# A recurrent attention and a gated feed-forward: inputs loaded by unit, smaller blocks at both ends, two fused operations

## The chip, the cores and the metric

The kernel runs on one core of one Trainium2 chip. The time is device time in microseconds (us) from launch to end. Before the change it is 272.43 us, the median of three runs (272.05 to 272.52). The core's engines each run their own stream of instructions in a fixed order: TensorE (PE; its weight loads are PEld), VectorE (DVE), ScalarE (ACT), GpSimd (POOL) and SyncE (SP), which issues transfers here; GpSimd issues the weight loads. An instruction waits at the head of its stream until the semaphores that it needs are set, and all that stands behind it in that stream waits too.

## The reference

```
# r, k, v, w: 4 x 8 heads x 768 steps x 48, float32; u: 8 x 48
for t in range(768):                       # for every batch and head
    cur   = outer(u * k[t], v[t])
    y[t]  = r[t] @ (state + cur)
    state = w[t][:, None] * state + outer(k[t], v[t])
x   = y as 3072 tokens x 384               # tokens of a batch in order, heads side by side
out = ((x @ w1) * (x @ w2)) @ w3 @ w_out   # 384 -> 1024 -> 1024 -> 384
```

## The kernel before, in words

Time is cut into chunks of 128 steps. A *unit* n is one chunk of one batch with all eight heads: there are 24 units, 6 for each of the 4 batches, and the state is handed from one unit of a batch to the next.

`prep` takes the logarithm of w (`lw`, on ScalarE) and a bf16 copy of v (`v_bf`, on GpSimd). `att_a` sums the logarithms along time with two triangular matrices on TensorE (`cs`, lines 137 to 139), takes the exponential of both sums (`e_sb`, line 140), multiplies k by the one and r by the other (`krt`, line 143, VectorE), transposes the eight pieces (`tr`, line 147) and copies them out of PSUM (`trs`, line 150). On GpSimd k, u and r are multiplied (`uk`, lines 153 and 154); VectorE sums over the head (`dsum`), and GpSimd multiplies that by v (`yd`): the part of a step with itself. `att_b` forms the 128 x 128 products of every head (`m`, line 174), masks them (`mbf`, line 177), forms the next state (`kv`, lines 183 and 186: two products a pair of heads, and behind each pair a one-column sum of the logarithms; then `pc`, `ts_`, `s_bd`, `s_f`), adds state and chunk parts into `y`, and transposes the result into `xT` (`yt`, lines 226 and 230).

The feed-forward works on blocks of four units (512 tokens). `ffn_ab` makes one group of 128 hidden columns: three matmuls into `a_ps`, three into `b_ps`, a copy of a on ScalarE and a product on VectorE into `abT` (line 250). `ffn_out` makes 128 tokens of the output with eight matmuls (`o_ps`) against `w34`, a copy and a store. `w34` is w3 @ w_out, made once in the kernel by `w34_transpose` (transposes of w3, lines 264 and 265) and `w34_mul` (line 270).

Loads: batch 0 comes chunk by chunk (24 loads of 192 KB on SP), batches 1 to 3 whole, four loads of 1.125 MB each, asked for at the first unit of the batch before, with two buffers for each input. GpSimd issues the weight loads, which turn float32 into bf16 on the way: w1 and w2 behind `att_a` of unit 0, w3 and w_out behind that of unit 1. `keep_in_program_order` pins each behind the GpSimd instruction written before it.

Order: the program writes units 0 to 3, then for each block j its feed-forward parts in four lots, with a unit of the next block ahead of each lot; for block 0 the making of w34 stands between a/b and out. The framework's scheduler then orders each engine's stream: of what its own model of the times takes to be ready it picks what was written first. So an instruction of a later unit can stand in a stream ahead of one of an earlier unit. Buffers bound how far ahead it gets: three for `lw`, `krt` and `v_bf`, two for most others.

PSUM has eight banks: three for the feed-forward (`ps_ffn`), two that `cs` (twice), `tr`, `kv` and `yt` share in turn (`ps_att`, tag att), two for the two halves of `m` (`ps_m`), one for `y`.

Of the kernel before, what the change touches and what calls it, by code (L numbers as in the profile page):

```python
# [14 lines left out]
def kernel(  # L15
# [48 lines left out]
    LT_incl = consts.tile([C, C], BF)  # L64
    LT_strict = consts.tile([C, C], BF)
# [34 lines left out]

    def load_batch(b, c0=0, c1=NC):
        for name, ap in (("w", w), ("k", k), ("r", r), ("v", v)):
            if c0 == 0:
                t = inp.tile([C, H, NC, D], F32, tag=name, name=f"{name}b", bufs=2)
                for c in range(NC):
                    ins[name, b, c] = t[:, :, c, :]
                bt[name] = t
            t = bt[name]
            if c1 - c0 == NC:
                nc.sync.dma_start(t.rearrange("t h c d -> t (h c) d"),  # L110
                                  ap[b].rearrange("h (c t) d -> t (h c) d", t=C))
            else:
                nc.sync.dma_start(t[:, :, c0, :], ap[b, :, c0 * C:c1 * C, :].rearrange("h t d -> t h d"))  # L113

    bt = {}
# [12 lines left out]

    state = {}

    def att_a(n):

        b, c = divmod(n, NC)
        lw = lws[n]
        v_bf = vbs[n]
# [100 lines left out]
    def ffn_ab(j, fi):  # L236
        if fi == 0:
            abts[j] = big.tile([P, FI, TB], BF, tag="abT", name=f"abT{j}")
        x = xts[j]
# [12 lines left out]
    def ffn_out(j, t):
# [6 lines left out]
        nc.sync.dma_start(out3[j * UPB + t], o_sb)

# [29 lines left out]
    def att(n):  # L290
        b, c = divmod(n, NC)
        if c == 0 and b + 1 < B:
            load_batch(b + 1)
# [2 lines left out]
        if n == 0:
            load_w(w1_bf, moe_w1)
            load_w(w2_bf, moe_w2)
        if n == 1:
            load_w(w3_bf, moe_w3)  # L300
            load_w(wo_bf, moe_w_out)
# [2 lines left out]
    fill = [lambda gi=gi: w34_transpose(gi) for gi in range(FI)] + \
           [lambda fi=fi: w34_mul(fi) for fi in range(FI)]
    for n in range(UPB):
        att(n)
    for j in range(NB):
        parts = [lambda fi=fi: ffn_ab(j, fi) for fi in range(FI)]
        if j == 0:  # L310
            parts += fill
        parts += [lambda t=t: ffn_out(j, t) for t in range(UPB)]
        units = [n for n in range((j + 1) * UPB, (j + 2) * UPB) if n < NU]
        k_ = 0
        for q in range(UPB):
            if q < len(units):
                att(units[q])
            e = len(parts) * (q + 1) // UPB
            while k_ < e:
                parts[k_]()  # L320
                k_ += 1


# [28 lines left out]
```

## Time and profile before

| | |
|---|---|
| median of three runs | 272.43 us |
| the profiled execution: time, span | 271.93 us, 270.2 us |
| mean granted clock of TensorE | 0.942 |
| busy: TensorE, VectorE, GpSimd, ScalarE | 204.8, 140.1, 111.6, 110.8 us |
| moved by DMA | 28.51 MB, mean 106 GB/s |

The span goes from the first to the last instruction; the time has the launch and the end around it. Busy is the time in which an engine has an instruction under way; matmuls are pipelined, so a busy TensorE is not one at its peak. The granted clock is the share of full speed that TensorE was given, with two levels, 1.2 and 2.4 GHz. Bytes of the weight loads count as they are written, in bf16.

### The profile page before, as it was taken

Reading aid. Unit: us, or ns where it says so; the run is one execution under the profiler, and the core shown is the slowest. Engines: PE = TensorE matmul, PEld = TensorE weight load, DVE = VectorE, ACT = ScalarE, POOL = GpSimd, SP = SyncE. Lnnn points to the kernel's source line nnn. Section 1 sums busy time; section 2 is a strip of 40 time slices with the busy share of each in tenths; the row PEclk is TensorE's granted clock in tenths of the full one; section 3 lists DMA queues with packets and bytes.
Section 4 is the critical chain, followed back from the end, with each engine's and each line's share of the span. In section 5 each row is a group of like instructions: output and inputs, shape, how many; then the busy total and the mean of one; then the engine's idle time right before and its main releaser. Section 6 shows DMA issues by size and latency. Waiting matters only on the chain.

```text
span 270.2 us, 4248 instructions
## 1 busy us (share of the span) xinstructions
PE 204.8 (76%) x1624; PEld 110.1 (41%) x1624; DVE 140.1 (52%) x246; ACT 110.8 (41%) x221; POOL 111.6 (41%) x152
## 2 busy tenths in 40 slices
PE   2460450359998859988897998959997699994994
PEld 1240230134465535534453444525454345552452
DVE  5340530543689323267776677666764646742340
ACT  3240210225444323345645564534655336442342
POOL 4762530861503953455474536754471313100000
PEclk9999999999999986999999999968999659996899
DMA  6999999999999992146919910300003000020003
GB/s 145 184 180 196 184 202 189 184 187 189 189 173 188 186 187 36 58 92 139 174 65 184 205 23 0 121 0 2 0 0 119 0 0 2 1 90 29 0 1 116
DMA packets 50084, 28.51 MB, mean 106 GB/s; under 512 B 25616, under 2 KB 48272, under 8 KB 50064
## 3 DMA queue, kind: packets, MB, share of 16 engines
q1 hardware_dynamic: 47184, 23.79, 45.2%
q0 software_dynamic: 2880, 4.46, 9.3%
q8 instruction: 12, 0.20, 0.3%
q14 instruction: 8, 0.07, 0.1%
HBM read 27.98 MB, written 4.72 MB: 121 GB/s over the span
## 4 chain that ended last, share of the span: by engine, by line
PE 48%; DVE 13%; POOL 10%; SPq 10%; DMA 9%; issue 4%; ACT 3%; POOLq 0%; ACTq 0%; DVEq 0%
PE a_ps L242 11%; PE b_ps L246 11%; SPq L113 10%; PE o_ps L255 8%; DMA vb<-in_v_dram 7%; DVE krt L143 5%; PE tr L147 4%; PE kv L183 3%; POOL yd L158 3%; DVE mbf L177 3%; POOL uk L154 2%; POOL uk L153 2%; PE m L174 2%; PE kv L186 2%; PE y L218 2%
## 5 line engine op out<-in xcount | busy, mean ns | idle before, releaser
L250 DVE TENSOR_TENSOR abT<-a_sb,b_ps 128x512 bf16<-128x512 f32 x48 | 32.9, 686 | 29.9 <-PE b_ps L246 27.4
L242 PE MATMUL a_ps<-xT,w_bf 128*128 128x512 bf16 x144 | 45.3, 415 | 0.7 <-ACT xT L230 0.6
L246 PE MATMUL b_ps<-xT,w_bf 128*128 128x512 bf16 x144 | 45.1, 404 | 0.4 <-ACT a_sb L249 0.4
L249 ACT COPY a_sb<-a_ps 128x512 f32<-128x512 f32 x48 | 28.2, 586 | 31.4 <-PE a_ps L242 30.2
L177 DVE TENSOR_TENSOR mbf<-m,mask 128x512 bf16<-128x512 f32 x48 | 30.8, 684 | 12.4 <-PE m L174 12.4
L150 ACT COPY trs<-tr 128x1024 bf16<-128x1024 bf16 x24 | 24.3, 1011 | 30.3 <-PE tr L147 27.4
L255 PE MATMUL o_ps<-w,abT 128*128 128x384 bf16 x192 | 36.6, 326 | 0.0
L153 POOL TENSOR_TENSOR uk<-kb,u_bc 128x384 f32<-128x384 f32 x24 | 26.4, 1104 | 18.6 <-DVE dsum L156 16.9
L156 DVE TENSOR_REDUCE dsum<-uk 128x8 f32<-128x384 f32 x24 | 13.2, 551 | 38.5 <-POOL uk L154 30.4
L147 PE MATMUL tr<-I,krt 128*128 128x128 bf16 x192 | 22.1, 248 | 11.1 <-DVE krt L143 10.7
L124 POOL CAST v_bf<-vb 128x384 bf16<-128x384 f32 x24 | 12.0, 504 | 41.5 <-DMA vb<-in_v_dram 19.4
L147 PEld LDWEIGHTS <-krt 128*128 128x128 bf16 x192 | 13.5, 109 | 36.4 <-DVE krt L143 33.5
L154 POOL TENSOR_TENSOR uk<-uk,rb 128x384 f32<-128x384 f32 x24 | 26.0, 1086 | 3.7 <-DMA rb<-in_r_dram 2.6
L140 ACT ACTIVATE e_sb<-cs 128x384 f32<-128x384 f32 x48 | 23.3, 496 | 4.5 <-PE cs L139 4.3
L218 PE MATMUL y<-v_bf,mbf 128*128 128x48 bf16 x192 | 13.7, 193 | 15.0 <-DVE mbf L177 15.0
L121 ACT ACTIVATE lw<-wb 128x384 bf16<-128x384 f32 x24 | 12.6, 525 | 28.5 <-DMA wb<-in_w_dram 28.5
L230 ACT COPY xT<-yt 128x384 bf16<-128x384 bf16 x24 | 11.5, 478 | 29.8 <-PE yt L226 29.7
L143 DVE TENSOR_TENSOR krt<-kb,e_sb 128x384 bf16<-128x384 f32 x24 | 15.6, 649 | 13.5 <-ACT e_sb L140 13.5
L158 POOL TENSOR_TENSOR yd<-v_bf,dsum 128x384 bf16<-128x384 bf16 x24 | 20.3, 846 | 5.0 <-DVE y_bf L223 4.3
L255 PEld LDWEIGHTS <-abT 128*128 128x128 bf16 x192 | 17.4, 97 | 10.6 <-DVE abT L250 0.2
L242 PEld LDWEIGHTS <-w_bf 128*128 128x128 bf16 x144 | 14.3, 104 | 17.9 <-issue 7.9
L183 PE MATMUL kv<-v_bf,krt 128*64 128x48 bf16 x160 | 19.6, 224 | 0.9 <-POOL v_bf L124 0.9
(100 smaller groups left out, 254.6 us busy)
## 6 DMA issues: line engine op xcount, KB each, us to landing
out_dram<-o_sb SPq DMA_DIRECT2D x24, 192.0 KB, 1.9
w_bf<-in_moe_w_dram POOLq DMA_DIRECT2D x1, 2048.0 KB, 15.2
w_bf<-in_moe_w_dram POOLq DMA_DIRECT2D x2, 768.0 KB, 9.8
wb<-in_w_dram SPq DMA_DIRECT2D x6, 192.0 KB, 4.8
kb<-in_k_dram SPq DMA_DIRECT2D x6, 192.0 KB, 7.6
rb<-in_r_dram SPq DMA_DIRECT2D x6, 192.0 KB, 6.4
vb<-in_v_dram SPq DMA_DIRECT2D x6, 192.0 KB, 5.0
wo_bf<-in_moe_w_out_dram POOLq DMA_DIRECT2D x1, 768.0 KB, 19.7
```

What stands on the lines that cost most here:

```text
L143: nc.vector.tensor_mul(krt[:, j, :, 0:D], ins["kr"[j], b, c], e_sb[:, j])
L147: nc.tensor.transpose(tr[:, j, p, :], krt[:, j, 2 * p:2 * p + 2, :].rearrange("t h d -> t (h d)"), I128)
L153: nc.gpsimd.tensor_mul(uk, ins["k", b, c], u_bc)
L154: nc.gpsimd.tensor_mul(uk, uk, ins["r", b, c])
L158: nc.gpsimd.tensor_mul(yd, v_bf, dsum[:, :, None].to_broadcast([C, H, D]))
L177: nc.vector.tensor_mul(mbf[:, q], mps[q], mask)
L183: nc.tensor.matmul(kv[q * DP:(q + 1) * DP, p, 0:D], lhsT=krt[:, 0, 2 * p + q, :], rhs=v_bf[:, 2 * p + q, :], start=True, stop=True)
L242: nc.tensor.matmul(a_ps, lhsT=w1_bf[:, di, fi * P:(fi + 1) * P], rhs=x[:, di, :], start=(di == 0), stop=(di == DI - 1))
L246: nc.tensor.matmul(b_ps, lhsT=w2_bf[:, di, fi * P:(fi + 1) * P], rhs=x[:, di, :], start=(di == 0), stop=(di == DI - 1))
L249: nc.scalar.copy(a_sb, a_ps)
L250: nc.vector.tensor_mul(abts[j][:, fi, :], a_sb, b_ps)
L255: nc.tensor.matmul(o_ps, lhsT=abts[j][:, fi, t * P:(t + 1) * P], rhs=w34[:, fi, :], start=(fi == 0), stop=(fi == FI - 1))
```

## The change

Inputs are loaded by unit: `load(n)` issues w, k, r and v of one unit into three tiles (k and r side by side in one), with eight buffers each. Units 0 to 7 are asked for at the start, unit n + 8 behind `att(n)`. w1 and w2 are issued behind unit 1's second `uk` product, w3 and w_out behind unit 3's, both under `high_priority`.

Blocks are lists of units: two of two units, four of four, two of two; the feed-forward of a block of two works on 256 columns. `big`, which holds `xT` and `abT`, gets three buffers.

The feed-forward parts form one list with an estimated cost each: a/b of blocks 0 and 1, w34, the outs of blocks 0 and 1, then a/b and out of each further block. Ahead of a part, units are written as long as their number is below 3 + (cost written so far)/4.1.

Both sums `cs` go into one tile of two banks (with -1 in the one triangle in place of the scale), one exponential and one product serve both. That tile and the `m` tile, now also of two banks, share one slot (`ps_m`, one buffer). `ps_att` keeps `tr`, `kv` and `yt`. The four one-column sums of `kv` stand behind its eight products.

```diff
-    NB = NTOK // TB
+    NIN = 8
+    BLOCKS = [(0, 2), (2, 4)] + [(n, n + 4) for n in range(4, NU - 4, 4)] + [(NU - 4, NU - 2), (NU - 2, NU)]
...
-    big = ctx.enter_context(tc.tile_pool(name="big", bufs=2))
+    big = ctx.enter_context(tc.tile_pool(name="big", bufs=3))
...
-    ps_m = ctx.enter_context(tc.tile_pool(name="ps_m", bufs=2, space=bass.MemoryType.PSUM))
+    ps_m = ctx.enter_context(tc.tile_pool(name="ps_m", bufs=1, space=bass.MemoryType.PSUM))
...
+    def load(n):
+        b, c = divmod(n, NC)
+
+        def src(ap):
+            return ap[b, :, c * C:(c + 1) * C, :].rearrange("h t d -> t h d")
+
+        w_in = inp.tile([C, H, D], F32, tag="w_in", name="w_in")
+        kr_in = inp.tile([C, 2, H, D], F32, tag="kr_in", name="kr_in")
+        v_in = inp.tile([C, H, D], F32, tag="v_in", name="v_in")
+        nc.sync.dma_start(w_in, src(w))
+        nc.sync.dma_start(kr_in[:, 0], src(k))
+        nc.sync.dma_start(kr_in[:, 1], src(r))
+        nc.sync.dma_start(v_in, src(v))
+        ins[n] = (w_in, kr_in, v_in)
...
+    def load_w(dst, ap):
+        with tc.high_priority():
+            d = nc.gpsimd.dma_start(dst, ap.rearrange("(i p) f -> p i f", p=P))
+        tc.keep_in_program_order(d)
...
-        for j, (lt, sc) in enumerate(((LT_incl, -1.0), (LT_strict, 1.0))):
-            cs = ps_att.tile([C, H, D], F32, tag="att")
-            nc.tensor.matmul(cs, lhsT=lt, rhs=lw[:, :, 0:D], start=True, stop=True)
-            nc.scalar.activation(e_sb[:, j], cs, Act.Exp, scale=sc)
+        cs = ps_m.tile([C, 2, TB], F32, tag="m", name="cs")
+        for j, lt in enumerate((LTn_incl, LT_strict)):
+            nc.tensor.matmul(cs[:, j, 0:DM], lhsT=lt, rhs=lw[:, :, 0:D], start=True, stop=True)
+        nc.scalar.activation(e_sb.rearrange("t j h d -> t j (h d)"), cs[:, :, 0:DM], Act.Exp)
         krt = kr_st[n % NS]
-        for j in range(2):
-            nc.vector.tensor_mul(krt[:, j, :, 0:D], ins["kr"[j], b, c], e_sb[:, j])
+        nc.vector.tensor_mul(krt[:, :, :, 0:D], kr_in, e_sb)
...
+        if n == 1:
+            load_w(w1_bf, moe_w1)
+            load_w(w2_bf, moe_w2)
+        if n == 3:
+            load_w(w3_bf, moe_w3)
+            load_w(wo_bf, moe_w_out)
...
-        mps = [ps_m.tile([C, HP, C], F32, tag="m", name=f"m{q}") for q in range(2)]
+        mps = ps_m.tile([C, 2, HP, C], F32, tag="m", name="mps")
...
+            for p in range(HP):
                 nc.tensor.matmul(kv[:, p, D:D + 1],
...
+        T = (BLOCKS[j][1] - BLOCKS[j][0]) * C
...
-    load_batch(0, 0, 1)
+    load(0)
     nc.sync.dma_start(u_bc, u.partition_broadcast(C))
-    for c in range(1, NC):
-        load_batch(0, c, c + 1)
+    for n in range(1, NIN):
+        load(n)
...
         att_b(n)
+        if n + NIN < NU:
+            load(n + NIN)
...
+    parts = []
+
+    def add_ab(j):
+        for fi in range(FI):
+            parts.append((1.3 * (BLOCKS[j][1] - BLOCKS[j][0]) / UPB, lambda fi=fi: ffn_ab(j, fi)))
+
+    def add_out(j):
+        for t in range(BLOCKS[j][1] - BLOCKS[j][0]):
+            parts.append((1.3, lambda t=t: ffn_out(j, t)))
+
+    add_ab(0)
+    add_ab(1)
+    for gi in range(FI):
+        parts.append((0.45, lambda gi=gi: w34_transpose(gi)))
+    for fi in range(FI):
+        parts.append((1.3, lambda fi=fi: w34_mul(fi)))
+    add_out(0)
+    add_out(1)
+    for j in range(2, len(BLOCKS)):
+        add_ab(j)
+        add_out(j)
+
+    lead, every = 3, 4.1
+    nxt, done = 0, 0.0
+    for cost, part in parts:
+        while nxt < NU and nxt < lead + done / every:
+            att(nxt)
+            nxt += 1
+        part()
+        done += cost
```

## Rows read from the trace of the kernel before

**Rows 1.** The page: busy us by engine; the chain that ended last, by engine.

```profile
PE 204.8 (76%) x1624; PEld 110.1 (41%) x1624; DVE 140.1 (52%) x246; ACT 110.8 (41%) x221; POOL 111.6 (41%) x152
...
PE 48%; DVE 13%; POOL 10%; SPq 10%; DMA 9%; issue 4%; ACT 3%; POOLq 0%; ACTq 0%; DVEq 0%
```

**Rows 2.** Windows by stage: window, its us, busy us by engine, PEclk, DMA share, GB/s.

```profile
0.00:64.00 64.00, 25.53 (x198) 14.78 (x198) 23.50 (x46) 15.58 (x31) 31.05 (x48) 1.00 1.10 183
108.00:208.00 100.00, 88.96 (x751) 47.19 (x750) 64.81 (x109) 52.25 (x106) 52.09 (x64) 0.97 0.34 79
12.00:28.00 16.00, 5.55 (x45) 3.27 (x45) 4.91 (x10) 3.50 (x7) 8.90 (x12) 1.00 1.12 186
28.00:48.00 20.00, 7.06 (x57) 4.16 (x58) 5.24 (x10) 2.86 (x6) 5.69 (x9) 1.00 1.18 195
48.00:96.00 48.00, 39.28 (x324) 22.23 (x323) 28.11 (x48) 20.00 (x40) 25.52 (x33) 1.00 1.05 184
180.00:200.00 20.00, 19.71 (x151) 9.68 (x150) 14.39 (x24) 11.33 (x24) 11.18 (x13) 0.89 0.00 1
```

**Rows 3.** Timeline, POOL: start us, us, engine, line, operation.

```profile
27.39 0.94 POOL L276 DMA_DIRECT2D w_bf<-in_moe_w_dram  x1
```

**Rows 4.** DMA issues: queue, count, KB each, median us to landing.

```profile
w_bf<-in_moe_w_dram POOLq DMA_DIRECT2D x2, 768.0 KB, 9.8
wo_bf<-in_moe_w_out_dram POOLq DMA_DIRECT2D x1, 768.0 KB, 19.7
```

**Rows 5.** Timeline, 26 to 51 us: waits of three engines, in brackets.

```profile
48.49 0.50 POOL L124 CAST v_bf<-vb 128x384 bf16<-128x384 f32 x1 [9.46 <-DMA vb<-in_v_dram]
49.70 0.52 ACT L121 ACTIVATE lw<-wb 128x384 bf16<-128x384 f32 x1 [13.90 <-DMA wb<-in_w_dram]
49.98 0.55 DVE L156 TENSOR_REDUCE dsum<-uk 128x8 f32<-128x384 f32 x1 [11.02 <-POOL uk L154]
```

**Rows 6.** Timeline, ACT: the 5th, 9th and 24th xT copy.

```profile
70.63 0.48 ACT L230 COPY xT<-yt 128x384 bf16<-128x384 bf16 x1 [0.66 <-PE yt L226]
...
120.14 0.48 ACT L230 COPY xT<-yt 128x384 bf16<-128x384 bf16 x1 [1.64 <-PE yt L226]
...
248.14 0.48 ACT L230 COPY xT<-yt 128x384 bf16<-128x384 bf16 x1 [3.56 <-PE yt L226]
```

**Rows 7.** Timeline, 138 to 146 us: one unit's cs, mbf, yt, next cs.

```profile
138.16 0.33 PE L139 MATMUL cs<-lw,LT_incl 128*128 128x384 bf16 x1
...
143.08 1.29 DVE L177 TENSOR_TENSOR mbf<-m,mask 128x512 bf16<-128x512 f32 x2 [1.99 <-PE m L174]
...
145.43 0.34 PE L226 MATMUL yt<-I,y_bf 128*128 128x128 bf16 x3 [0.65 <-DVE y_bf L223]
...
145.61 0.33 PE L139 MATMUL cs<-lw,LT_incl 128*128 128x384 bf16 x1
```

**Rows 8.** Timeline, PE: the first a_ps, the last b_ps and o_ps.

```profile
60.58 1.49 PE L242 MATMUL a_ps<-xT,w_bf 128*128 128x512 bf16 x3
...
260.29 0.81 PE L246 MATMUL b_ps<-xT,w_bf 128*128 128x512 bf16 x3
260.94 5.36 PE L255 MATMUL o_ps<-w,abT 128*128 128x384 bf16 x32
```

**Rows 9.** Timeline, PE, 225 to 230 us: kv and m in a dense stretch.

```profile
226.06 0.21 PE L183 MATMUL kv<-v_bf,krt 128*64 128x48 bf16 x2
...
227.00 0.38 PE L242 MATMUL a_ps<-xT,w_bf 128*128 128x512 bf16 x1
...
228.97 0.40 PE L174 MATMUL m<-trs 48*128 48x128 bf16 x8
229.30 0.34 PE L213 MATMUL y<-sbd,trs 128*128 128x96 bf16 x4
```

**Rows 10.** The page's groups: line, engine, operation, shapes, count, busy us, mean ns.

```profile
L249 ACT COPY a_sb<-a_ps 128x512 f32<-128x512 f32 x48 | 28.2, 586 | 31.4 <-PE a_ps L242 30.2
...
L140 ACT ACTIVATE e_sb<-cs 128x384 f32<-128x384 f32 x48 | 23.3, 496 | 4.5 <-PE cs L139 4.3
```

More of the change, by code (lines that the diff above doesn't have):

```diff
@@ L55 @@
     stat = ctx.enter_context(tc.tile_pool(name="static", bufs=1))
-    inp = ctx.enter_context(tc.tile_pool(name="inp", bufs=3))
+    inp = ctx.enter_context(tc.tile_pool(name="inp", bufs=NIN))
     work = ctx.enter_context(tc.tile_pool(name="work", bufs=2))
-    big = ctx.enter_context(tc.tile_pool(name="big", bufs=2))
+    big = ctx.enter_context(tc.tile_pool(name="big", bufs=3))
     ps_ffn = ctx.enter_context(tc.tile_pool(name="ps_ffn", bufs=3, space=bass.MemoryType.PSUM))
     ps_att = ctx.enter_context(tc.tile_pool(name="ps_att", bufs=2, space=bass.MemoryType.PSUM))
-    ps_m = ctx.enter_context(tc.tile_pool(name="ps_m", bufs=2, space=bass.MemoryType.PSUM))
+    ps_m = ctx.enter_context(tc.tile_pool(name="ps_m", bufs=1, space=bass.MemoryType.PSUM))
     ps_y = ctx.enter_context(tc.tile_pool(name="ps_y", bufs=1, space=bass.MemoryType.PSUM))
-    LT_incl = consts.tile([C, C], BF)
+    LTn_incl = consts.tile([C, C], BF)
     LT_strict = consts.tile([C, C], BF)
@@ L72 @@
     nc.vector.memset(ones_c, 1.0)
-    nc.gpsimd.memset(LT_incl, 1.0)
-    nc.gpsimd.affine_select(LT_incl, LT_incl, compare_op=Alu.is_ge, fill=0.0,
+    nc.gpsimd.memset(LTn_incl, -1.0)
+    nc.gpsimd.affine_select(LTn_incl, LTn_incl, compare_op=Alu.is_ge, fill=0.0,
                             base=0, channel_multiplier=-1, pattern=[[1, C]])
@@ L99 @@
     ins = {}
[L101 to L115, printed above, removed]
+    def load(n):
[10 more added lines that the diff above has]
+        ins[n] = (w_in, kr_in, v_in)
     vbs = {}
     def prep(n):
-        b, c = divmod(n, NC)
         lw = lw_st[n % NS]
-        nc.scalar.activation(lw[:, :, 0:D], ins["w", b, c], Act.Ln)
+        nc.scalar.activation(lw[:, :, 0:D], ins[n][0], Act.Ln)
         lws[n] = lw
         v_bf = work.tile([C, H, D], BF, tag="v_bf", bufs=3)
-        nc.gpsimd.tensor_copy(v_bf, ins["v", b, c])
+        nc.gpsimd.tensor_copy(v_bf, ins[n][2])
         vbs[n] = v_bf
     lws = {}
+    def load_w(dst, ap):
+        with tc.high_priority():
+            d = nc.gpsimd.dma_start(dst, ap.rearrange("(i p) f -> p i f", p=P))
+        tc.keep_in_program_order(d)
     state = {}
@@ L173, in att_b @@
                 o = q * DP
-                nc.tensor.matmul(mps[q][:, p, :], lhsT=trs[o:o + D, 0, p, :],
+                nc.tensor.matmul(mps[:, q, p, :], lhsT=trs[o:o + D, 0, p, :],
                                  rhs=trs[o:o + D, 1, p, :], start=True, stop=True)
         for q in range(2):
-            nc.vector.tensor_mul(mbf[:, q], mps[q], mask)
+            nc.vector.tensor_mul(mbf[:, q], mps[:, q], mask)
         if c < NC - 1:
@@ L226, in att_b @@
             nc.tensor.transpose(yt[:, di, :], y_bf[:, di * P:(di + 1) * P], I128)
-        j, qd = divmod(n, UPB)
-        if qd == 0:
+        j = next(i for i, (lo, hi) in enumerate(BLOCKS) if lo <= n < hi)
+        lo, hi = BLOCKS[j]
+        if n == lo:
             xts[j] = big.tile([P, DI, TB], BF, tag="xT", name=f"xT{j}")
-        nc.scalar.copy(xts[j][:, :, qd * C:(qd + 1) * C], yt)
+        nc.scalar.copy(xts[j][:, :, (n - lo) * C:(n - lo + 1) * C], yt)
     xts = {}
@@ L239, in ffn_ab @@
         x = xts[j]
+        T = (BLOCKS[j][1] - BLOCKS[j][0]) * C
         a_ps = ps_ffn.tile([P, TB], F32, tag="f", name="a_ps")
         for di in range(DI):
-            nc.tensor.matmul(a_ps, lhsT=w1_bf[:, di, fi * P:(fi + 1) * P], rhs=x[:, di, :],
+            nc.tensor.matmul(a_ps[:, 0:T], lhsT=w1_bf[:, di, fi * P:(fi + 1) * P], rhs=x[:, di, 0:T],
                              start=(di == 0), stop=(di == DI - 1))
@@ L245, in ffn_ab @@
         for di in range(DI):
-            nc.tensor.matmul(b_ps, lhsT=w2_bf[:, di, fi * P:(fi + 1) * P], rhs=x[:, di, :],
+            nc.tensor.matmul(b_ps[:, 0:T], lhsT=w2_bf[:, di, fi * P:(fi + 1) * P], rhs=x[:, di, 0:T],
                              start=(di == 0), stop=(di == DI - 1))
         a_sb = work.tile([P, TB], F32, tag="a_sb")
-        nc.scalar.copy(a_sb, a_ps)
-        nc.vector.tensor_mul(abts[j][:, fi, :], a_sb, b_ps)
+        nc.scalar.copy(a_sb[:, 0:T], a_ps[:, 0:T])
+        nc.vector.tensor_mul(abts[j][:, fi, 0:T], a_sb[:, 0:T], b_ps[:, 0:T])
     def ffn_out(j, t):
@@ L258, in ffn_out @@
         nc.scalar.copy(o_sb, o_ps)
[L259 removed]
+        nc.sync.dma_start(out3[BLOCKS[j][0] + t], o_sb)
     def w34_transpose(gi):
@@ L290, in att @@
     def att(n):
-        b, c = divmod(n, NC)
-        if c == 0 and b + 1 < B:
-            load_batch(b + 1)
         prep(n)
         att_a(n)
[L296 to L301, printed above, removed]
-        att_b(n)
[L304 to L321, printed above, removed]
+        att_b(n)
+        if n + NIN < NU:
[26 more added lines that the diff above has]
+        done += cost
 _INS = ['r', 'k', 'v', 'w', 'u', 'moe_w1', 'moe_w2', 'moe_w3', 'moe_w_out']
```

8 lines of the change are left out of this document (3 added, 5 removed).

## The prediction

> **What bounds the kernel now.** I read the page first, then windows by stage, then single stretches. TensorE is the busiest engine, but at 204.8 of 270.2 us far from full, and the chain that ended last lies only 48% on it [rows 1]. The windows show where it stands idle: it is busy 25.53 us of the first 64, beside DMA at 183 GB/s, and 89% from 108 to 208 [rows 2]. So there are different limits by stage.
>
> *Head, 0 to 60 us: loads.* DMA runs at 183 to 195 GB/s throughout [rows 2]. Weights take most of it while they are in flight: from 28 to 48 us 20 us x 195 GB/s = 3.9 MB moved; w3 and w_out, issued from 27.39 us and landed up to 19.7 us later [rows 3, 4], are 2.9 MB as bf16, so unit loads got 1.0 MB, a quarter. Work is then held up by order: ScalarE sat 13.90 us until a w landed at 49.70, for the Ln of a later unit, and could do nothing that stood behind it; GpSimd sat 9.46 us for a v, and behind it VectorE's dsum 11.02 us [rows 5]. The first a_ps starts at 60.58 us [rows 8]: a block of four units must be there before any feed-forward work.
>
> *Middle, 60 to 248 us: the chain of one unit.* The 5th, 9th and 24th xT copy come at 70.63, 120.14 and 248.14 us [rows 6]: 12.4 us a unit up to the 9th, while batch 1 is still loading, then 128.0/15 = 8.53. One unit shows why [rows 7]: cs at 138.16, the mbf products end at 143.08 + 1.29 = 144.37, yt at 145.43, and only then the next unit's cs, at 145.61. Units run one behind the other; feed-forward matmuls fill the holes, but not wholly. TensorE's own work: 512 columns take 0.216 us from start to start (three in 0.65), 384 take 0.163 (32 in 5.2, without the last one's tail) [rows 8]. So a/b 288 x 0.216 = 62.2, out 192 x 0.163 = 31.3, w34 64 x 0.163 + 64 x 0.054 (a third, for 128 columns) = 13.9: 107.4 us of feed-forward, 15.6 a block of four units, 3.9 a unit. One unit of attention with its 20 feed-forward matmuls is 57 matmuls; 751 of them kept TensorE busy 88.96 us in 108 to 208 [rows 2], 6.75 us for 57, so attention is some 2.7 us a unit at a clock of 0.97. 6.75 stands against the 8.53 that a unit takes.
>
> *Tail, 248 to 270 us:* after the 24th xT come 16 groups of a/b, 32 o_ps, a copy and a store, 22.0 us [rows 6, 8].
>
> **The change, part by part.**
>
> *Loads by unit.* 0.786 MB a unit instead of 4.72 a batch; at 190 GB/s 4.1 us. The pieces in memory are as short as before (one head's 192 bytes). Chunk loads beside weights moved 186 GB/s (12 to 28 us); 48 to 96, when batch loads ran, shows 184 [rows 2]: I take no change of rate, with 6% either way by the spread of these rows. The Trainium skill speaks against this part: "DMA: Bandwidth & Descriptors", section Bandwidth, asks for loads of 1 MiB or more and has 341 GB/s there and 138 at 64 KB; its ratio would make 184 GB/s some 75 (an estimate from that page), and the time some 289 us, as in rival 4. The trace does not agree: both forms stand at one rate.
>
> *Weights later.* w1 and w2 are pinned behind unit 1's second uk product, w3 and w_out behind unit 3's. u and two units are 1.8 MB, in by 11 us; the products end at 13, and w1, w2 land 9.8 us after issue [rows 4], at 23 to 24. Unit 2 has a quarter of the rate until then, is whole at 26, unit 3 at 30. w3, w_out go in at 31 and land at 51 (19.7 us [rows 4]); a quarter of the rate puts unit 4 at 43, unit 5 at 53, and then 4.1 us each. On SP the first 32 loads wait for no slot. Loads 8 and on stand in one queue with the stores and wait for products that free their slot; they have eight units' slack, so I cost that at nothing.
>
> *Blocks of two units at the ends.* The first a/b needs units 0 and 1 only. If ScalarE, VectorE and GpSimd keep an order as in rows 5, a unit ends some 4.5 us after the next one's data (the half of the loop of rows 7 behind krt): unit 1's xT at 30.5, unit 2's at 37, unit 3's at 48, unit 4's at 58, then one each 7 us, unit 7's at 79. Block 0 (5.2 us of matmuls) runs at 30.5, block 1 at 48, w34 from 51. From 54 us on TensorE always has something: w34 and two blocks' outs, 19 us, then units 4 to 7. At the end 16 groups of 256 columns and 16 o_ps follow the last xT: 5.2 + 2.6 us, 2.5 of evacuation and low clock, and 3.9 from the last matmul to the end (266.3 to 270.2 [rows 8]): 14.2 instead of 22.0. Sixteen more copies and products cost their fixed part, 0.2 us each (by rows 10), on engines under 55% busy: nothing; without that cover 3 us.
>
> *Attention further ahead; one two-bank tile for cs and m.* The list of feed-forward work is no longer tied to the block that attention works on, so the holes at block ends go. Five uses of two banks (cs, cs, tr, kv, yt) become three, so cs need not wait for yt; but cs and m now share one slot: the next unit's cs waits for both mbf products of this one. That loop, cs to end of mbf, is late next: 6.2 us in rows 7; the 16 units from the 9th on repeat the pattern with 6.1 to 7.7 and one of 9.0 at low clock. Behind the waiting cs on TensorE stands the feed-forward work that the order put there, and it waits too. I take 7.2 us a unit; worst 8.53 (nothing won), best 6.5 (TensorE's own work).
>
> *Fused exponential and product.* Two exponentials of 496 ns become one: 586 ns for 512 columns against 496 for 384 [rows 10] is 0.7 ns a column and 0.23 us fixed, so 0.77 us, 0.2 less a unit on ScalarE. VectorE saves one fixed part likewise. On the chain the first product no longer runs under the second exponential, so between 0.3 us lost and 0.2 won a unit; I take 0.
>
> *kv sums behind the kv products.* In a dense stretch these 12 matmuls take 0.94 us, eight m take 0.33 [rows 9]. Grouped, 0.4 (at the m pace) to 0.94; I take 0.65, 0.3 us less a unit.
>
> **Sum.** From 54 us: feed-forward 107.4 - 10.4 (blocks 0 and 1) = 97.0; attention 19.5 units x 2.4 = 46.8; together 144. At the granted clock of 0.97 [rows 2] 148. Idle share: 11% from 108 to 208, where the unit chain bound; 1.5% from 180 to 200 [rows 2]. I take 8%: 161. 54 + 161 + 3.9 = 219. The attention loop would allow 79 + 16 x 7.2 + 14.2 = 208, so TensorE sets the end. The profiled execution took 271.93 us for a span of 270.2, and the median of the three runs is 272.43, 2.2 above the span: 221. Most errors of the head make it later, so I say 223.
>
> **Rivals.**
> 1. *The unit chain still binds*, because cs, tr and m wait behind feed-forward matmuls, or because the streams are ordered so that the lead isn't there: 8.53 us a unit as now, 58 + 19 x 8.53 + 14.2 + 2.2 = 236; with unit 4 later by 8 us, 244. For it: this is what bounds today. Against: the 1.24 us from mbf's end to the next cs [rows 7] leave the loop.
> 2. *TensorE nearly full:* idle 2%, kv at 0.4 us: (144 - 5)/0.97/0.98 = 146, and 54 + 146 + 3.9 + 2.2 = 206. For it: 19.71 of 20 us busy in 180 to 200 [rows 2]. Against: at a clock of 0.89 there, and everywhere else fixed orders stalled.
> 3. *Slower: the shared slot.* If the mbf products stand in VectorE's queue behind a later unit's dsum that waits for GpSimd, as it did for 11.02 us [rows 5], the next cs stands still too, now without a second slot. It decides at (272.4 - 58 - 14.2 - 2.2)/19 = 10.4 us a unit; at the 12.4 of the 5th to 9th unit now the time is 310. Against: data is in well ahead after 60 us, and the longest loop seen is 9.0.
> 4. *Chunk loads come slower.* At 80 GB/s: 18.9 MB in 236 us, 24 for weights, 14 for the end: 274; at 75, 290. Rows 2 have no such stretch.
>
> **Chances.** Forecast (215 to 231) 0.51; rival 1 (231 to 247) 0.26; rival 2 (205 to 215) 0.12; 247 to 271, a later head, 0.04; rivals 3 and 4 0.05 and 0.02, a little of it at no change. Range 208 to 246. With 0.2% (0.5 us) as what a measurement of this kernel can tell: faster 0.93, same 0.01, slower 0.06.
>
> **What would show it.** First a_ps near 30 us and w34 from some 51; DMA near 190 GB/s until the units are in; the last 16 xT copies 7.2 us apart, with cs right behind mbf and no longer behind yt; TensorE over 90% busy from 54 us on; under 15 us from the last xT to the end. A first a_ps after 40 us, or units over 8.5 us apart, makes it wrong.

## The result, and the profile after

The changed kernel takes 225.53 us (median of four runs, 225.03 to 226.69), the kernel before, run beside it, 272.24. The ratio is 0.8302 (95% interval 0.825 to 0.8354). The profiled execution took 225.09 us for a span of 223.4, at a mean granted clock of 0.977. 223 was forecast. Three executions of the kernels tried below ran over 1.5% slower than the fastest of the same kernel (243.75 of the third in the table, 229.49 and 230.02 of the fifth), so the medians of these two are too high.

The page: busy us by engine, the DMA packets, the chain that ended last by engine.

```profile
PE 176.8 (79%) x1720; PEld 103.5 (46%) x1720; DVE 133.1 (60%) x238; ACT 108.9 (49%) x213; POOL 115.4 (52%) x152
...
DMA packets 106342, 28.54 MB, mean 128 GB/s; under 512 B 100304, under 2 KB 104528, under 8 KB 106320
...
PE 39%; SPq 14%; DMA 14%; POOL 13%; DVE 8%; issue 7%; ACT 3%; POOLq 0%; DVEq 0%; ACTq 0%
```

Against [rows 1] TensorE is busy 28 us less and is still a larger part of a shorter span; GpSimd and the loads have gained in the chain. Of the 28 us the grouped kv sums give some 12 (20 units x 0.59, below). Another part is the clock: the kernel before ran partly at 1.2 GHz in four stretches behind 98 us (98 to 107, 176 to 186, 210 to 223, 244 to 254 us; granted 0.61 to 0.66, TensorE busy 33.8 us in them), the changed one in one (46 to 59 us; 0.61, 5.5 us busy). The windows tell where (columns as in [rows 2]):

```profile
12.00:28.00 16.00, 6.10 (x72) 4.17 (x73) 6.60 (x12) 4.29 (x8) 10.85 (x14) 1.00 1.14 190
28.00:48.00 20.00, 13.95 (x142) 9.14 (x140) 8.94 (x18) 8.24 (x18) 8.79 (x13) 0.98 1.16 190
48.00:64.00 16.00, 10.05 (x97) 6.98 (x98) 10.29 (x22) 6.22 (x14) 12.12 (x17) 0.70 1.13 191
54.00:108.00 54.00, 47.15 (x518) 29.65 (x518) 36.16 (x65) 26.79 (x55) 41.78 (x50) 0.97 1.09 176
54.00:223.40 169.40, 154.14 (x1494) 89.16 (x1493) 109.37 (x191) 92.27 (x182) 86.67 (x108) 0.99 0.58 109
108.00:208.00 100.00, 95.28 (x893) 51.31 (x892) 69.00 (x117) 60.14 (x114) 44.89 (x59) 1.00 0.38 82
```

TensorE does 13.95 us of work from 28 to 48 where it did 7.06, and from 108 to 208 it runs 893 matmuls where it ran 751. Transfers by unit move 190 GB/s beside the weights, as large ones did [rows 2], though there are twice the packets. One stretch is poor: 48 to 64 us, with a clock of 0.70. TensorE stood idle for 6.31 us up to 50.52, waiting for mbf; the clock fell in that wait and is at 0.50, the lower level, from 48 to 57 us.

The 4th, 9th and 24th xT copy (to [rows 6]), and TensorE's first a_ps, last b_ps and last o_ps (to [rows 8]), from the timelines of ScalarE and TensorE:

```profile
54.04 0.47 ACT L243 COPY xT<-yt 128x384 bf16<-128x384 bf16 x1
94.35 0.47 ACT L243 COPY xT<-yt 128x384 bf16<-128x384 bf16 x1
199.58 0.48 ACT L243 COPY xT<-yt 128x384 bf16<-128x384 bf16 x1
```

```profile
32.28 0.80 PE L256 MATMUL a_ps<-xT,w_bf 128*128 128x256 bf16 x3 [0.57 <-ACT xT L243]
...
216.53 0.49 PE L260 MATMUL b_ps<-xT,w_bf 128*128 128x256 bf16 x3
216.94 2.76 PE L269 MATMUL o_ps<-w,abT 128*128 128x384 bf16 x16
```

The feed-forward starts 28 us earlier. A unit takes (199.58 - 94.35)/15 = 7.02 us instead of 8.53. From the last xT to the end pass 23.8 us, more than before.

The head is held up once, and its rows answer to [rows 3 to 5] (GpSimd's issue of w3, and waits from 45 to 54 us; w3 lands 15.6 us after its issue, w_out 20.1):

```profile
30.05 0.94 POOL L131 DMA_DIRECT2D w_bf<-in_moe_w_dram  x1
```

```profile
46.75 0.99 POOL L158 TENSOR_TENSOR uk<-kr_in,u_bc 128x384 f32<-128x384 f32 x1 [6.77 <-DMA kr_in<-in_k_dram]
47.70 0.99 POOL L159 TENSOR_TENSOR uk<-uk,kr_in 128x384 f32<-128x384 f32 x1
48.72 0.55 DVE L167 TENSOR_REDUCE dsum<-uk 128x8 f32<-128x384 f32 x1 [6.95 <-POOL uk L159]
49.78 1.28 DVE L188 TENSOR_TENSOR mbf<-mps,mask 128x512 bf16<-128x512 f32 x2
...
52.92 0.52 ACT L121 ACTIVATE lw<-w_in 128x384 bf16<-128x384 f32 x1 [9.23 <-DMA w_in<-in_w_dram]
```

GpSimd waits 6.77 us for the k of unit 5 (this is its sixth first product, L158), which the weights delay. The second product of unit 4 (47.70, the fifth of L159) stands behind it, so VectorE's dsum of unit 4 waits too, with the mbf products of unit 3 (49.78) behind that in its queue, and unit 3's xT comes at 54.04.

One unit of the middle (timeline, to [rows 7, 9]): kv, then the loop through mbf to the next cs.

```profile
140.89 0.31 PE L194 MATMUL kv<-v_bf,krt 128*64 128x48 bf16 x8
141.13 0.25 PE L198 MATMUL kv<-ones_c,lw 128*128 128x1 bf16 x4
141.24 0.38 PE L256 MATMUL a_ps<-xT,w_bf 128*128 128x512 bf16 x1
...
142.78 1.28 DVE L188 TENSOR_TENSOR mbf<-mps,mask 128x512 bf16<-128x512 f32 x2
...
144.31 0.32 PE L145 MATMUL cs<-lw,LTn_incl 128*128 128x384 bf16 x1
...
145.28 0.33 PE L238 MATMUL yt<-I,y_bf 128*128 128x128 bf16 x3
```

The next cs starts 0.25 us behind the end of mbf (144.06) and ahead of yt. The twelve kv matmuls take 0.35 us from their start to the next matmul; they took 0.94.

### The profile page after: what moved, and what is told of

It is laid out like the page before. It is cut to its first block, busy times and chain, and to the rows that moved or that the text cites. A ratio compares the mean times of both kernels' runs of the same rounds, so it can differ in the third digit from the quotient of the medians.

```text
span 223.4 us, 4564 instructions
## 1 busy us (share of the span) xinstructions
PE 176.8 (79%) x1720; PEld 103.5 (46%) x1720; DVE 133.1 (60%) x238; ACT 108.9 (49%) x213; POOL 115.4 (52%) x152
## 2 busy tenths in 40 slices
DMA packets 106342, 28.54 MB, mean 128 GB/s; under 512 B 100304, under 2 KB 104528, under 8 KB 106320
## 4 chain that ended last, share of the span: by engine, by line
PE 39%; SPq 14%; DMA 14%; POOL 13%; DVE 8%; issue 7%; ACT 3%; POOLq 0%; DVEq 0%; ACTq 0%
DMA v_in<-in_v_dram 9%; PE b_ps L260 9%; PE a_ps L256 8%; PE o_ps L269 7%; DVE krt L148 7%; SPq L113 6%; PE tr L152 5%; POOL yd L169 4%; DMA kr_in<-in_k_dram 4%; SPq L114 3%; POOL sbd L211 3%; SPq L112 3%; SPq L111 2%; POOL uk L159 2%; PE mps L185 2%
## 5 line engine op out<-in xcount | busy, mean ns | idle before, releaser
L264 DVE TENSOR_TENSOR abT<-a_sb,b_ps 128x256 bf16<-128x256 f32 (+1 forms) x64 | 35.0, 549 | 23.2 <-ACT a_sb L263 11.8
L256 PE MATMUL a_ps<-xT,w_bf 128*128 128x256 bf16 (+1 forms) x192 | 45.6, 333 | 3.6 <-ACT xT L243 2.4
L260 PE MATMUL b_ps<-xT,w_bf 128*128 128x256 bf16 (+1 forms) x192 | 45.4, 332 | 2.3 <-ACT a_sb L263 1.8
L263 ACT COPY a_sb<-a_ps 128x256 f32<-128x256 f32 (+1 forms) x64 | 30.6, 481 | 23.2 <-PE a_ps L256 22.5
L158 POOL TENSOR_TENSOR uk<-kr_in,u_bc 128x384 f32<-128x384 f32 x24 | 29.3, 1221 | 23.5 <-DMA kr_in<-in_k_dram 11.8
L148 DVE TENSOR_TENSOR krt<-kr_in,e_sb 128x768 bf16<-128x768 f32 x24 | 27.2, 1132 | 12.0 <-ACT e_sb L146 12.0
L188 DVE TENSOR_TENSOR mbf<-mps,mask 128x512 bf16<-128x512 f32 x48 | 30.8, 682 | 3.1 <-PE mps L185 2.8
L146 ACT ACTIVATE e_sb<-cs 128x768 f32<-128x768 f32 x24 | 19.5, 811 | 21.0 <-PE cs L145 20.9
L159 POOL TENSOR_TENSOR uk<-uk,kr_in 128x384 f32<-128x384 f32 x24 | 26.3, 1096 | 1.6
L256 PEld LDWEIGHTS <-w_bf 128*128 128x128 bf16 x192 | 18.1, 100 | 11.5 <-issue 2.7
L260 PEld LDWEIGHTS <-w_bf 128*128 128x128 bf16 x192 | 18.2, 99 | 10.4 <-issue 3.0
L121 ACT ACTIVATE lw<-w_in 128x384 bf16<-128x384 f32 x24 | 12.7, 529 | 19.9 <-DMA w_in<-in_w_dram 19.9
L230 PEld LDWEIGHTS <-mbf 128*128 128x128 bf16 x192 | 9.4, 98 | 22.1 <-DVE mbf L188 20.3
## 6 DMA issues: line engine op xcount, KB each, us to landing
w_bf<-in_moe_w_dram POOLq DMA_DIRECT2D x1, 2048.0 KB, 15.6
wo_bf<-in_moe_w_out_dram POOLq DMA_DIRECT2D x1, 768.0 KB, 20.1
```

The lines of the kernel that those rows point to most:

```text
L148: nc.vector.tensor_mul(krt[:, :, :, 0:D], kr_in, e_sb)
L158: nc.gpsimd.tensor_mul(uk, kr_in[:, 0], u_bc)
L159: nc.gpsimd.tensor_mul(uk, uk, kr_in[:, 1])
L188: nc.vector.tensor_mul(mbf[:, q], mps[:, q], mask)
L256: nc.tensor.matmul(a_ps[:, 0:T], lhsT=w1_bf[:, di, fi * P:(fi + 1) * P], rhs=x[:, di, 0:T], start=(di == 0), stop=(di == DI - 1))
L260: nc.tensor.matmul(b_ps[:, 0:T], lhsT=w2_bf[:, di, fi * P:(fi + 1) * P], rhs=x[:, di, 0:T], start=(di == 0), stop=(di == DI - 1))
```

## The experiments

Times of different chips differ by up to 1%, so each kernel is set against the kernel before on its own chip. "Cost" is the ratio less 0.8302, times 272.2 us; two intervals enter into it, so it is uncertain by about 3 us, and by about 4 where so marked. Medians and ranges hold all runs.

The last column is the mean granted clock of TensorE in each kernel's runs; the changed kernel has 0.962 to 0.977, the kernel before 0.942 to 0.948. The lower it is, the longer TensorE ran at 1.2 GHz, so a cost in this table holds what the clock took as well. In the head of every kernel the rows give 1.00 although matmuls take as long there as at the lower level (in the changed kernel the cs at 4.47 us takes 0.48 us, the one at 144.31 takes 0.32), so these means leave the head out.

| kernel | us (range) | ratio, 95% | cost, us | clock |
|---|---|---|---|---|
| kv sums mixed again | 232.86 (232.54-233.36) | 0.856 [0.8523, 0.8598] | 7.0 | 0.967-0.978 |
| two exps, two products | 241.93 (239.93-242.42) | 0.8878 [0.8825, 0.8931] | 15.7 | 0.933-0.942 |
| the same, cs in the att banks | 241.44 (239.78-243.75) | 0.8854 [0.8792, 0.8915] | 15.0 | 0.942-0.970 |
| two exps, one product, cs in the att banks | 244.55 (244.29-245.61) | 0.9049 [0.8994, 0.9104] | 20.3 | 0.923-0.930 |
| two exps, one product | 227.91 (225.95-230.02) | 0.8459 [0.8354, 0.8564] | 4.3 (+-4) | 0.963-0.977 |
| one exp, two products | 235.15 (234.79-236.01) | 0.8733 [0.8684, 0.8781] | 11.7 | 0.956-0.963 |
| old way of writing the units | 233.12 (231.71-234.21) | 0.8562 [0.8503, 0.8621] | 7.1 | 0.946-0.960 |
| first block of four | 230.76 (230.37-232.2) | 0.8541 [0.8485, 0.8597] | 6.5 | 0.999-1.000 |
| last block of four | 224.46 (223.94-224.99) | 0.8299 [0.8249, 0.8348] | -0.1 | 0.961-0.977 |
| w3 and w_out later | 225.68 (224.1-227.27) | 0.8324 [0.826, 0.8389] | 0.6 | 0.953-0.976 |
| batches 1 to 3 loaded whole | 234.49 (234.02-235.14) | 0.8705 [0.8657, 0.8753] | 11.0 | 0.949-0.963 |
| kernel before, kv sums grouped | 259.7 (258.07-260.24) | 0.9629 [0.9568, 0.9689] | -10.1 against before | 0.960-0.967 |

**The kv sums**, mixed again with the kv products: the one line `for p in range(HP):` is taken out.

> The changed kernel with one thing undone: each one-column sum of kv stands again behind its pair of kv products. Theory A (TensorE's own work sets the end from 54 us on): the twelve kv matmuls take 0.94 us again instead of the 0.35 us they take grouped (140.89 to 141.24 us in the changed kernel), 0.59 x 20 units = 12 us of TensorE work in the filled stretch, so 225.5 + 8 to 12 = 233 to 238 us. Theory B (the loop of one unit, cs to mbf, sets the pace): kv runs while ScalarE copies trs for 1.0 us, so nothing: 225 to 227 us.

7.0 us, a little under the 8 to 12 of the first theory. Everything behind 54 us in this kernel, against 154.14 us of TensorE in 169.40 in the changed one:

```profile
54.00:230.90 176.90, 164.24 (x1494) 97.85 (x1492) 109.63 (x190) 93.71 (x180) 85.74 (x107) 0.97 0.55 104
```

TensorE is busy 10.1 us more, and the stretch is 7.5 us longer; its idle time there falls from 15.3 to 12.7 us. So three quarters of the added work show. That TensorE's work alone is the bound does not follow, since the same edit lengthens the chain of a unit: m stands behind kv on TensorE, and beyond the usual 0.06 us behind the copy of trs it is 14.5 us late in all, against 4.4 in the changed kernel. This edit cannot tell work and chain apart.

**The same line in the kernel before**:

> The kernel before with the one-column sums of kv grouped behind the eight kv products, nothing else. In the changed kernel this grouping is worth 7.3 us. Theory B (it is worth time only where TensorE is the bound; before, a unit's chain binds, and kv stands on TensorE beside ScalarE's copy of trs, which hides it): 270 to 273 us. Rival: 20 units x 0.59 us = 12 us of TensorE time fall away, and at least half shows: 260 to 266 us.

10.1 us faster: the rival was right, and "worth time only where TensorE is the bound" falls. The timeline of the kernel before shows what I had missed:

```profile
157.85 0.21 PE L183 MATMUL kv<-v_bf,krt 128*64 128x48 bf16 x2
157.96 1.01 ACT L150 COPY trs<-tr 128x1024 bf16<-128x1024 bf16 x1 [1.24 <-PE tr L147]
...
158.76 0.18 PE L186 MATMUL kv<-ones_c,lw 128*128 128x1 bf16 x1
158.80 0.81 PE L242 MATMUL a_ps<-xT,w_bf 128*128 128x512 bf16 x3
159.44 0.38 PE L246 MATMUL b_ps<-xT,w_bf 128*128 128x512 bf16 x1
159.75 0.40 PE L174 MATMUL m<-trs 48*128 48x128 bf16 x8
```

The copy of trs ends at 158.97, but m stands behind kv and four feed-forward matmuls, and starts 0.78 us later. In 8 of the 24 units m started over 0.3 us behind the copy, 8.2 us in all beyond the usual 0.06; with the sums grouped that lateness is 3.6 us in all. So up to 4.6 us of the ten lay on the chain of a unit there. Another part is the clock. In the kernel before it falls to the lower level around 177 us, behind a chain in which TensorE waited again and again, and three matmuls of 512 columns then take 1.49 us, where they take 0.81 at 158.80:

```profile
176.00:186.00 10.00, 7.45 (x57) 3.94 (x59) 5.28 (x9) 4.37 (x10) 5.03 (x6) 0.66 0.00 0
```

```profile
181.00 1.49 PE L242 MATMUL a_ps<-xT,w_bf 128*128 128x512 bf16 x3
```

By the mean clocks of the profiled runs, 0.942 and 0.966, some 31 of 270 us and 18 of 258 us were at the lower level (an estimate from these means and the spans, the head left out). How the ten us divide between chain, clock and TensorE's own work no run here shows.

**Both fusions undone**, slot kept:

```diff
-        nc.scalar.activation(e_sb.rearrange("t j h d -> t j (h d)"), cs[:, :, 0:DM], Act.Exp)
+        for j in range(2):
+            nc.scalar.activation(e_sb[:, j].rearrange("t h d -> t (h d)"), cs[:, j, 0:DM], Act.Exp)
...
-        nc.vector.tensor_mul(krt[:, :, :, 0:D], kr_in, e_sb)
+        for j in range(2):
+            nc.vector.tensor_mul(krt[:, j, :, 0:D], kr_in[:, j], e_sb[:, j])
```

> The changed kernel with two exponentials and two products again, cs still in the shared two-bank slot. Theory A (TensorE's work sets the end): its work is the same, ScalarE and VectorE have 0.2 us a unit more and are under 60% busy: 225 to 227 us. Theory B (the unit's loop sets the pace): the first product runs under the second exponential again, the loop is up to 0.3 us shorter or, with two fixed parts more, 0.2 us longer: 20 x that, 219 to 230 us, and not the same.

15.7 us slower, beyond both. Two kernels undo one half each. First the exponentials alone:

> The changed kernel with two exponentials of 384 columns in place of the one of 768; slot and single product stay. The two stretches of time that the unfused kernels lost (16 us with both fusions undone) must come from the exponentials, from the products, or from the order of the streams that the split brings. In this kernel cs stands behind the y group and ahead of yt for 22 of 24 units, as in the changed kernel (21). Theory P (the second product costs, because it waits beside GpSimd's uk): nothing but ScalarE's fixed part, 0.2 us a unit, off the bound: 224 to 228 us. Rival E (the exponentials carry it: the product can only start behind the second, 0.3 us a unit later, and the chain of a unit takes it over): 231 to 236 us.

Theory P's range holds it: 227.91 us, and the two lower times, 225.95 and 226.33, would make the cost 2.5 us; it can't be told from nothing. Then the products alone:

> The changed kernel with two products of 384 columns into krt in place of the one of 768; slot and single exponential stay. cs again stands ahead of yt for 21 of 24 units. Theory P: the second product meets GpSimd's uk and waits, 0.6 us of VectorE a unit on the chain from cs to tr, as with both fusions undone (1.72 against 1.13 us a unit): 0.6 x 15 to 24 units = 9 to 14 us, so 234 to 240 us. Rival O (what the unfused kernels lost came from the order of the streams, not from the products): 225 to 229 us.

Theory P: 11.7 us. Timelines of VectorE and GpSimd, first of the changed kernel, then of this one:

```profile
152.50 0.55 DVE L167 TENSOR_REDUCE dsum<-uk 128x8 f32<-128x384 f32 x1 [0.97 <-POOL yd L169]
152.97 0.95 DVE L148 TENSOR_TENSOR krt<-kr_in,e_sb 128x768 bf16<-128x768 f32 x1
153.13 1.64 POOL L158 TENSOR_TENSOR uk<-kr_in,u_bc 128x384 f32<-128x384 f32 x1 [0.67 <-DVE dsum L167]
```

```profile
138.74 1.82 DVE L148 TENSOR_TENSOR krt<-kr_in,e_sb 128x384 bf16<-128x384 f32 x2
138.90 1.24 POOL L158 TENSOR_TENSOR uk<-kr_in,u_bc 128x384 f32<-128x384 f32 x1 [0.67 <-DVE dsum L167]
```

dsum releases both: VectorE goes on to krt, and GpSimd 0.16 us later to the next uk. In the changed kernel the one product ends after 0.95 us, and uk, 1.00 us when alone, takes 1.64: it ends 0.85 us behind krt. With two products the first (0.55 us when alone) is through by 139.29; then uk has its turn until 140.14, and only then the second product ends, at 140.56. So the split puts a GpSimd instruction between two halves of the chain from cs to tr. The groups over the whole run, changed kernel first:

```profile
L148 DVE TENSOR_TENSOR krt<-kr_in,e_sb 128x768 bf16<-128x768 f32 x24 | 27.2, 1132 | 12.0 <-ACT e_sb L146 12.0
```

```profile
L148 DVE TENSOR_TENSOR krt<-kr_in,e_sb 128x384 bf16<-128x384 f32 x48 | 37.5, 821 | 11.8 <-ACT e_sb L146 11.7
```

10.3 us more VectorE time, and the kernel ends 9.6 us later by the medians. So of the 15.7 us of both fusions the product has the most; the rest, 4.0 us, is the exponentials' and too small here to be split from the error. TensorE's work is the same in these kernels, so its work does not set the time alone: VectorE's part of a unit's chain does too.

**cs back in the att banks**, one bank each, m in two banks, exponentials and products unfused:

```diff
-        cs = ps_m.tile([C, 2, TB], F32, tag="m", name="cs")
...
+            cs = ps_att.tile([C, H, D], F32, tag="att")
...
-        mps = ps_m.tile([C, 2, HP, C], F32, tag="m", name="mps")
+        mps = [ps_m.tile([C, HP, C], F32, tag="m", name=f"m{q}") for q in range(2)]
```

> As the unfused one, and cs in the two banks that tr, kv and yt share, m in two banks of its own, as in the kernel before; loads, blocks, lead and kv stay as changed. Theory A1 (freeing cs from yt is what let the units run 7.0 instead of 8.5 us apart): cs again behind yt, 8.5 us a unit from 63.5 us on, 24th xT at 225, time 237 to 243 us. Rival A2 (lead and kv grouping gave the pace, the banks nothing): units stay 7 us apart, 225 to 229 us.

The time is in the range of A1, but equal to that of the unfused kernel that keeps the slot: the banks by themselves gave nothing there. Then the same with the one product:

> The changed kernel with cs back in the two banks of tr, kv and yt, m in its own two banks, two exponentials, but one product for k and r. Two products took 1.72 us a unit where one takes 1.13, since the second waits behind a GpSimd uk that starts between them (the unfused run). Theory P (the one product is what the fusion was worth, the banks nothing): 225 to 230 us. Theory S (the banks count too, once the product is one): units 0.6 us closer than the 8.2 us of the run with cs in att, 7.6 us, and so 231 to 236 us.

Neither: 20.3 us. Here cs stands behind yt again for every unit, and GpSimd is there first (timeline):

```profile
145.43 1.00 POOL L158 TENSOR_TENSOR uk<-kr_in,u_bc 128x384 f32<-128x384 f32 x1 [0.67 <-DVE dsum L167]
...
145.89 1.35 DVE L148 TENSOR_TENSOR krt<-kr_in,e_sb 128x768 bf16<-128x768 f32 x1
```

With two exponentials and one product the slot is worth some 16 us (cost 20.3 against 4.3); with two products it is worth nothing (241.44 against 241.93). So the two edits pay only together: from two products in the att banks (cost 15.0), the slot alone gives nothing, the single product alone loses 5 us, both gain some 11.

Why is not shown. With the slot cs comes ahead of yt, and the single product is then more often ahead of uk; but VectorE's krt products take 29.7 us in all in this kernel against 27.2 in the changed one, a small part of 16 us, and with two products in the att banks they take 37.7 us and the kernel is no slower. The clock has a part as well: it is lowest here, at 0.66 from 156 to 166 us and 0.61 from 187 to 200. With two products the slot does bring the last xT forward (213.46 against 225.26 us in the profiled runs), but 24.7 us of work follow it there, and 16.8 without the slot.

**The lead**: the units are written as before, one ahead of each lot of a block's parts (blocks of two kept).

> The changed kernel with the old way of writing units: those of the next block spread in equal lots over the parts of this one, no lead of three; blocks, banks, loads and kv as changed. Theory A (a lead only fills the holes at block ends): four holes of 1 to 2 us and a later start of some units, 229 to 234 us. Rival (the lead is what lets TensorE be full): units at the end of each block bind as before, 8.5 us a unit, 237 to 243 us.

As the first theory had it. The last units come late (timeline, the fourth from the end and the last xT copy; in the changed kernel they were over at 199.58):

```profile
190.81 0.48 ACT L243 COPY xT<-yt 128x384 bf16<-128x384 bf16 x1 [0.85 <-PE yt L238]
...
219.00 0.48 ACT L243 COPY xT<-yt 128x384 bf16<-128x384 bf16 x1 [0.42 <-PE yt L238]
```

**The small blocks**, first those at the start (`BLOCKS = [(n, n + 4) for n in range(0, NU - 4, 4)] + ...`, four units written ahead):

> The changed kernel with a first block of four units instead of two of two (units 0 to 3 are written ahead of the first part). Theory A (TensorE is full from 54 us on, before that it waits for loads): the first a_ps comes at 54 us instead of 32, and what is lost is block 0's 5.2 us of matmuls that then fall into the full stretch: 229 to 232 us. Rival (the early start is worth its 22 us): 240 to 247 us.

6.5 us, as expected; the first a_ps waits for unit 3, and takes as long as at the lower clock:

```profile
58.17 1.44 PE L256 MATMUL a_ps<-xT,w_bf 128*128 128x512 bf16 x3 [0.76 <-ACT xT L243]
```

Then those at the end (`BLOCKS = [(0, 2), (2, 4)] + [(n, n + 4) for n in range(4, NU, 4)]`):

> The changed kernel with a last block of four units instead of two of two. Theory A (TensorE has older feed-forward work until 203 us, the 24th xT is there at 199.6, and the sum of work is the same): 224 to 227 us. Rival (the small blocks shorten the tail by the 7.8 us worked out in the prediction): 231 to 234 us.

Nothing lost: at the end units are so far ahead that feed-forward work is always there, whatever the size of the last block.

**w3 and w_out later** (`if n == 5:` in place of 3):

> The changed kernel with w3 and w_out issued behind unit 5's uk instead of unit 3's. Theory A (TensorE lacks data until 54 us, since w3 and w_out take three quarters of the rate from 30 to 51): unit 4's data lands near 36 us instead of 46, the 4th xT comes near 43 instead of 54, block 1 and the block of units 4 to 7 fill TensorE before w34: 217 to 222 us. Rival (the outs of blocks 0 and 1 hold the two abT buffers until w34 is made, so work only changes places): 225 to 229 us.

The rival. The 4th xT comes at 46.25 us instead of 54.04, but the next stretch loses what that gave (window of this kernel, against 47.15 us at a clock of 0.97):

```profile
54.00:108.00 54.00, 42.05 (x433) 26.94 (x431) 29.90 (x53) 23.05 (x45) 34.90 (x41) 0.85 1.08 174
```

The wait moves to a later unit (GpSimd, its ninth first product, so the k of unit 8):

```profile
64.11 0.99 POOL L158 TENSOR_TENSOR uk<-kr_in,u_bc 128x384 f32<-128x384 f32 x1 [6.21 <-DMA kr_in<-in_k_dram]
```

The dsum of unit 8 waits behind it, and behind that the mbf products of unit 5, whose xT comes at 71.61 instead of 70.25. In the changed kernel it was unit 5's k that held unit 3; the expectation's account by unit 4's data was not right. TensorE also ran at a clock of 0.85 in this window.

**Whole batches**, as before the change, from batch 1 on:

> The changed kernel with the inputs of batches 1 to 3 loaded whole, as before the change (batch 0 by unit; batch 1 is asked for behind unit 0, two buffers; to fit, y_bf has one buffer in place of two). Theory L (the order of arrival sets the first third): unit 6, the first of batch 1, is complete only when two batches and the weights are in, 9.4 MB + 6.0 MB at 190 GB/s = 81 us, its xT at some 88 in place of 79, and TensorE stands idle for most of the difference: 232 to 242 us. Rival (TensorE has block 0, block 1 and w34 to do until then, so a later unit 6 costs nothing): 224 to 228 us.

11.0 us, theory L. GpSimd waits for the whole batch (timeline; the "x2" are two units at once), and two windows tell what TensorE lacks:

```profile
66.06 2.13 POOL L161 TENSOR_TENSOR uk<-kr_in,u_bc 128x384 f32<-128x384 f32 x2 [5.39 <-DMA kr_in<-in_k_dram]
72.29 1.96 POOL L162 TENSOR_TENSOR uk<-uk,kr_in 128x384 f32<-128x384 f32 x2 [4.10 <-DMA kr_in<-in_r_dram]
```

```profile
54.00:108.00 54.00, 46.69 (x471) 29.50 (x472) 32.03 (x58) 25.00 (x51) 33.13 (x43) 0.88 0.99 186
108.00:160.00 52.00, 43.30 (x415) 22.67 (x420) 34.89 (x60) 28.26 (x54) 36.21 (x43) 1.00 0.52 105
```

The changed kernel ran 518 and 456 matmuls in these. Unit 6's xT came at 83.71 us (79.21 in the changed kernel), not at 88, so only a part is the late unit itself. Behind 80 us nothing waits for an input any more; the rest may be the single buffer of y_bf, the smaller lead, or the clock (0.88 from 54 to 108 us, where the changed kernel had 0.97); that was not tried apart.

No kernel here beats the changed one by more than the measurement can tell.

## Why the prediction was near, step by step

- *Bound and stages: right in the main.* The head is set by arrival of data. From 54 us TensorE is the nearest to full (idle 9%, from 108 to 208 us 4.7%), but it does not set the end alone: two products in place of one add nothing to its work and cost 11.7 us.
- *No change of rate: right.* 190 GB/s in the loads by unit; rival 4 did not come. The Trainium skill's rule that loads should be 1 MiB or more ("DMA: Bandwidth & Descriptors", Bandwidth) has no hold here: 192 KB loads and 1.1 MB loads move the same, in pieces that are equally short in memory.
- *Order of arrival: right in mechanism, short by 6 us.* w1 and w2 were issued at 12.96 (13 forecast), w3 at 30.05 (31), the first a_ps came at 32.28 (30.5). xT of units 2 and 3 came at 40.35 and 54.04, forecast 37 and 48. The term that failed is unit 3's: I took a fixed 4.5 us behind the next unit's data, but unit 3's mbf stood in VectorE's queue behind unit 4's dsum, and that through GpSimd's queue behind the k of unit 5, used at 46.75. The data themselves came as forecast: the v of unit 5, its last input, at 52.19, forecast 53. Later units caught up: unit 7's xT at 85.89, forecast 79, and after it 7 us each.
- *Pace 7.2: measured 7.02*, with cs behind mbf as forecast. But the step "fused exponential and product: I take 0" is wrong by some 16 us. I weighed only ScalarE's and VectorE's own fixed parts (0.2 us) and did not ask who else wants VectorE's inputs at that time; and I credited the slot alone with the pace. Slot and single product give it together. With the slot and without the fusions the time is 241.93, in the range of rival 1 (231 to 247), though with units 7.7 us apart and not 8.53. That the pace came out as forecast is in part luck.
- *kv 0.65 us: measured 0.35*, below the lower bound of 0.4; 0.59 us a unit instead of 0.29. The bound came from the pace of m, whose moving side has 128 columns; kv's has 48 and 1.
- *Attention, 2.7 us a unit: miscounted.* 1624 matmuls less the 608 of the feed-forward are 1016, 42 a unit, so a unit with its 20 feed-forward matmuls has 62 and not 57. The same row then gives 88.96 x 62/751 = 7.3 us a unit, and attention 3.3 instead of 2.7. (89% of 8.53 us, 7.6 us, would have told.) Over 19.5 units that is 12 us too little; the kv saving, taken as 0.3 and measured as 0.59, takes back 6 of them. Measured: (154.14 - 97.0 - 5.2)/20 = 2.6 us a unit, against 2.4 in the sum. So this term came near by luck.
- *From 54 us: near.* Forecast 148 us of TensorE work with 8% idle; measured 154.14 busy of 169.40, 9% idle. Block 1's a/b, 5.2 us, still lay ahead at 54 us. The smaller kv and a clock of 0.99 (0.97 forecast) took back a part of what this, the miscount and the late head cost, so errors of both signs met: 223.4 us of span against 219, and 2 for launch and end.
- *Tail 14.2 us: beside the point.* The last xT is no longer the start of a tail. 23.8 us follow it, and in 200 to 217 us TensorE is busy without a gap. The sum used TensorE and not the tail, so nothing is lost by it; but the small last blocks, costed as a gain there, are worth nothing. The 3.9 us from the last matmul to the end are 223.4 - 219.70 = 3.7.
- *Rivals 2 and 3:* idle 2% did not come, since waits remain in the head and to 108 us (87% busy); from 108 to 208 it is 4.7%. The shared slot never stood still for long: the longest distance of xT copies behind the 9th is 8.5 us.

## What to carry to other kernels

Before an element-wise product is costed at its fixed part, look at which instruction of GpSimd starts beside it: on a chain, one long product can be worth far more than two half ones (11.7 us here), because a GpSimd instruction can step in between the halves. Two edits can be worth nothing, or less, apart and some 11 us together, so a PSUM slot and a fusion on one chain are best tried in all combinations. Work taken off the busiest engine shows only in part (0.59 us a unit, 12 us in all, showed as 7), and can show as much where that engine is not full (10), since an engine's stream also lies on the chain. A part that shortens the tail shows nothing once that engine has a backlog. A count of instructions, and the busy share times the time of a unit, check each other.

## What the runs showed of the hardware that was not expected

- A VectorE product of two SBUF tensors and a GpSimd product shut each other out; whoever starts first goes through. krt of 768 columns: 0.95 us when first, 1.35 behind a uk; uk: 1.00 us when first, 1.64 behind a krt. The Trainium skill states such an exclusive lock, decided by the order of issue ("SBUF — State Buffer", Who interferes with whom); these rows agree.
- The kv matmuls, 8 of 48 columns and 4 of one column, take 0.94 us when a one-column matmul on 128 rows of lw follows each pair, and 0.35 us when the kinds are grouped. What in the switch costs 0.15 us a pair no run here shows.
- Packets twice as many and half as large (106342 against 50084 for the same 28.5 MB) carried the same 190 GB/s in the loads.
